# Attention into a mixture of experts: softmax exponentials head by head on ScalarE in the first ten chunks, with new opening plans

## The chip, the cores and the metric

One core of a Trainium2 chip runs the whole program. The metric is device time in microseconds (us) of one execution. Five engines work side by side, each through its own list of instructions: TensorE (PE), VectorE (DVE), ScalarE (ACT), GpSimd (POOL) and SyncE (SP), whose queue issues most DMA transfers.

## What is computed

For each of 8 batches, 8 heads of 576 queries attend to 72 keys and values, which are means over 8 neighbours:

```python
k_p = k.reshape(B, H, Sp, pool, D).mean(axis=3)
v_p = v.reshape(B, H, Sp, pool, D).mean(axis=3)
scores = scale * np.matmul(q, k_p.transpose(0, 1, 3, 2))
scores = scores - np.max(scores, axis=-1, keepdims=True)
attn = np.exp(scores)
attn = attn / (np.sum(attn, axis=-1, keepdims=True) + 1e-09)
return np.matmul(attn, v_p)
```

The 4608 rows of 512 numbers then go through a mixture of experts. A router picks one of 4 groups and one of 4 experts in it for each row, the row goes through that expert alone, `relu(x @ w1) @ w2` with 1024 hidden units, and the result is scaled by the two router weights.

## The kernel before

The work is cut into batches, and a batch's 576 rows into 5 chunks (four of 128 rows and one of 64). While the expert layer of batch b runs, the attention of batch b+1 is made ready, and the loads of batch b+2 start. Nearly all rows of a batch go to one expert, whose weights are loaded whole; the few other rows are done at the end in blocks of 32, one block straight in the last plan and the rest in a loop, which may run zero times.

The order of all work is written by hand in four strings of pieces: `START` and `FIRST` (batch 0 and the attention of batch 1), `STEADY` (used for batches 1 to 6) and `LAST`. A piece such as `a.ex:2` is a method call: `a` is the attention of the current batch, `n` of the next, `x` of the one after, `m` and `w` are the expert layers of the current and next batch, `t` is filler, `l` the leftover rows. Each engine runs its instructions in list order. The built order, taken per engine, can put a piece that is ready early ahead of a neighbour in the string.

The pieces of one attention chunk, with their lines:
- `sc` (L335): PE forms the scores of 8 heads, 72 columns each, in the PSUM tile `sc`, of which there is one buffer (two banks).
- `mx` (L341): DVE takes the maximum of every head. `sb` (L348 in batch 0, two instructions of L352 later): DVE subtracts it and writes `p` to SBUF, which sets `sc` free. `ex` (L357): ACT takes the exponential of all 576 columns at once. `su_` (L362 to L364): DVE sums each head, adds 1e-9 and inverts.
- `nm` (L372, L375): POOL multiplies by the inverse, first for `px` (16 keys of every second head), then for all of `p`.
- `px_`, `pm` (L380, L399): PE transposes; `pxa`, `pma` (L385, L387, L404): ACT copies them, rounded, to `pr` and `ph`; `pxd`, `pmd` (L392, L408): DVE forms the remainders.
- `av` (L417): PE multiplies with the values, for a half of the batch (chunks 0 and 1, or 2 to 4) at a time; `ava`, `avd` (L420, L424): ACT and DVE store result and remainder in `xt`.

The expert layer: `m.load` (L583) brings a tile of weights, `m.split` (L590, ACT) rounds it, `m.spd` (L595, POOL or DVE) takes the remainder; `m.up` (L608) is 12 matmuls, `ua` (L613, ACT) and `upd` (L618, DVE) empty its PSUM; `m.down` (L647) is 8 matmuls, `da` (L660) scales and stores. In the last batch `m.half` (L627) does one chunk in two halves; the first is emptied and stored by ACT, the second by DVE (L633) and SP's queue (L634).

`t.warm:z` (L920) is z matmuls whose result nobody reads, to keep PE busy while it would wait. `l.fetch_a`, `l.fetch_b` and `l.fetch_x` (L822, L827, L818) are SP's ten loads for the next block of leftover rows; they have a condition in a register and move nothing where no block follows. `l.slots` (L778 to L795) is DVE's preparation of that block, and `l.down` ends in an indirect store by POOL (L883).

Of the kernel before, what the change touches and what calls it, by code (L numbers as in the profile page):

```python
# [34 lines left out]
a.load_r:v a.load_k:1:w a.kr:1:v t.warm:1 a.load_k:0:w t.load_wr a.load_v:0 a.kr:0:p t.warm:7 a.load_r:k a.load_v:1 a.load_q:0 a.vr:0:v a.rr:v  # L35
t.warm:11 a.load_q:1 t.warm:20 n.load_r:v a.kb a.vr:1:v a.kt n.load_r:k a.kta a.guess_x a.load_q:2 a.qt:0 a.qta:0 a.vmain a.guess_e a.sc:0 a.rcopy
m.load:1:1 a.qt:1 t.warm:2 a.vrem a.qta:1 a.qt:2 a.sc:1 a.mx:0 a.sb:0 a.ex:0 a.su_:0 a.nm:0:p a.mx:1 t.warm:4 a.vm:0 a.vrx a.sb:1 a.load_q:3 a.px_:0
m.load:1:3 a.pxa:0 a.vm:1 a.pm:0 a.pma:0 t.warm:1 t.warm:5 a.pxd:0 a.ex:1 a.pmd:0 a.av:1:0:128 a.av:2:0:128 m.load:1:2 a.av:0:0:128 a.su_:1 a.qta:2
a.ava:1:0:128 a.ava:2:0:128 a.ava:0:0:128 a.avd:1:0:128 a.avd:0:0:128 a.av:3:0:128 n.load_k:0 m.load:1:0 n.load_k:1 a.nm:1:p n.load_v:0 a.ava:3:0:128
m.split:1:1 a.sc:2 t.warm:1 a.pm:1 a.avd:3:0:128 a.load_q:4 a.mx:2 n.load_qb:2 a.px_:1 n.load_qb:0 a.qt:3 a.pxa:1 t.warm:3 a.avd:2:0:128 a.pma:1  # L40
a.sb:2 a.ex:2 a.pxd:1 m.split:1:0 a.pmd:1 m.spd:1:0:p a.su_:2 a.av:2:128:128 a.qta:3 a.ava:2:128:128 a.av:0:128:128 a.sc:3 n.load_qb:3 a.ava:0:128:128
a.av:1:128:128 a.av:3:128:128 a.ava:1:128:128 a.ava:3:128:128 a.avd:2:128:128 a.avd:0:128:128 a.avd:3:128:128 a.avd:1:128:128 m.up:0:0 m.spd:1:1:v
# [3 lines left out]
a.mx:4 a.pma:2 a.sb:4 a.ex:4 a.pmd:2 m.up:2:0 m.split:1:3 t.warm:3 m.up:4:0 m.ua:2:0 a.nm:3:p m.load:2:1 a.pm:3 m.load:2:0 m.upd:1:0 a.px_:3 a.su_:4
a.nm:4:p m.ua:4:0 a.pxd:2 m.up:3:0 a.pxa:3 a.px_:4 a.pma:3 a.pxa:4 a.pxd:3 m.upd:2:0 a.pmd:3 a.pm:4 a.pxd:4 a.pma:4 m.split:2:1 a.pmd:4 a.av:3:256:320
a.av:2:256:320 m.upd:4:0 m.ua:3:0 a.ava:2:256:320 n.load_qb:1 x.load_k:0 a.ava:3:256:320 m.split:2:0 m.up:5:0 m.spd:1:3:v a.av:1:256:320 x.load_r:v
a.av:0:256:320 a.avd:2:256:320 a.ava:1:256:320 n.kr:0:r m.up:6:0 a.ava:0:256:320 a.avd:1:256:320 a.avd:3:256:320 m.ua:6:0 n.rr:p n.kr:1:p m.ua:5:0
m.spd:2:0:p m.load:2:2 a.avd:0:256:320 a.rt m.upd:3:0 m.upd:6:0 n.kt m.up:1:1 n.kta n.qb:0 m.upd:5:0 n.load_v:1 n.qb:1 n.sc:0 m.up:7:0 a.route  # L50
m.load:2:3 n.mx:0 n.rcopy n.sb:0 n.qb:2 m.ua:7:0 a.count n.ex:0 m.spd:2:1:p n.su_:0 m.ua:1:1 n.sc:1 n.nm:0:p m.up:0:1 n.mx:1 m.up:2:1 n.vrem m.ua:0:1
m.upd:7:0 a.gex n.sb:1 n.sc:2 m.upd:0:1 n.ex:1 m.upd:1:1 n.su_:1 n.px_:0 n.pm:0 n.mx:2 m.up:3:1 n.pxa:0 n.nm:1:p m.ua:2:1 m.up:4:1 x.load_k:1 m.ua:3:1
n.qb:3 n.px_:1 n.sb:2 x.load_qb:2 n.ex:2 n.pxd:0 x.load_r:k n.qb:4 m.split:2:2 m.upd:2:1 n.pxa:1 n.vrx a.gates n.pm:1 n.sc:3 n.vr:1:p n.mx:3 m.up:5:1
# [918 lines left out]
```

## Time and profile before

| | |
|---|---|
| median of 3 runs | 576.86 us (576.35 to 577.75) |
| the profiled execution's own time | 574.12 us |
| its span, first to last instruction | 572.4 us |
| mean granted TensorE clock | 0.990 of full speed |
| batches 1 to 6, each | 64.6 us |

The span is what the views below describe, from 0 to 572.4 us. The profiled execution took 1.7 us more than its span, and 2.7 us less than the median of the other runs. The opening (`START`) reaches to the first expert matmul at 35.4 us, `FIRST` to about 116 us; then the same 64.6 us come six times.

### The profile page before, as it was taken

What the parts mean: (1) busy time and instruction counts of PE and PEld (TensorE: products, weight loads), DVE (VectorE), ACT (ScalarE), POOL (GpSimd) and SP (SyncE); (2) the same over time, 40 slices, a digit from 0 to 9 for tenths busy, and PEclk for the clock granted to TensorE, in tenths of its full rate; (3) what the DMA queues carried; (4) which work ended last, traced back from release to release, by engine and by line L of the source; (5) the groups of instructions that cost most, each with busy time, mean ns of one, the idle gap of its engine ahead of it and who ended that gap; (6) DMA issues with size and microseconds to landing.
All of it is one profiled execution on the core that took longest, in us unless ns stands there. A gap on an engine that the chain in (4) does not pass through costs nothing. (4 is left out here: it accounts for less than half of the span.)

```text
span 572.4 us, 13094 instructions
## 1 busy us (share of the span) xinstructions
PE 558.0 (97%) x4896; PEld 497.4 (87%) x4896; DVE 397.5 (69%) x1075; ACT 273.9 (48%) x621; POOL 302.5 (53%) x301
## 2 busy tenths in 40 slices
...
GB/s 214 198 211 206 59 120 66 222 116 219 93 122 185 111 177 56 223 76 206 107 117 191 113 174 56 223 236 187 95 97 211 74 2 19 238 84 89 386 69 44
DMA packets 119362, 81.45 MB, mean 142 GB/s; under 512 B 76790, under 2 KB 95990, under 8 KB 118912
## 3 DMA queue, kind: packets, MB, share of 16 engines
...
q14 instruction: 26, 0.21, 0.1%
...
## 5 line engine op out<-in xcount | busy, mean ns | idle before, releaser
L608 PE MATMUL mm<-xt,w 128*128 128x320 f32 (+1 forms) x1536 | 221.1, 300 | 0.8 <-DVE ht L618 0.5
L608 PEld LDWEIGHTS mm<-xt,w 128*128 128x128 f32 x1536 | 208.2, 190 | 2.6 <-issue 0.7
L647 PE MATMUL mm<-w,ht 128*128 128x512 f32 x744 | 180.1, 395 | 0.0
L647 PEld LDWEIGHTS mm<-w,ht 128*128 128x128 f32 x744 | 136.9, 188 | 29.5 <-issue 1.8
L595 POOL TENSOR_TENSOR w<-sw,w 128x1024 fp32r<-128x1024 f32 x47 | 113.4, 2429 | 36.1 <-ACT w L590 36.1
L613 ACT ACTIVATE ht<-mm 128x320 fp32r<-128x320 f32 (+1 forms) x128 | 50.0, 410 | 61.9 <-PE mm L608 60.7
L618 DVE SCALAR_TENSOR_TENSOR ht<-mm,ht 128x256 fp32r<-128x256 f32 (+1 forms) x192 | 60.3, 348 | 24.7 <-ACT ht L613 23.8
L660 ACT ACTIVATE y<-mm,gm 128x512 f32<-128x512 f32 x31 | 21.2, 684 | 105.1 <-PE mm L647 105.1
L590 ACT CAST w<-sw 128x1024 fp32r<-128x1024 f32 x64 | 65.7, 1049 | 8.1 <-DMA sw<-in_moe_w_dram 8.1
L372 POOL TENSOR_TENSOR px<-p,su 128x128 f32<-128x128 f32 (+1 forms) x40 | 17.1, 427 | 67.7 <-DVE su L364 58.1
L272 POOL TENSOR_TENSOR rp<-rp,rh 32x128 f32<-32x128 f32 x8 | 3.6, 454 | 90.8 <-DMA rp<-rp 74.3
L431 POOL TENSOR_TENSOR sw<-xt 128x256 f32<-128x256 f32 (+1 forms) x56 | 43.7, 806 | 13.3 <-DVE xt L424 13.2
L375 POOL TENSOR_TENSOR p<-p,su 128x576 f32<-128x576 f32 (+1 forms) x40 | 46.0, 1151 | 3.1
L424 DVE TENSOR_TENSOR xt<-tp,xt 128x320 fp32r<-128x320 f32 (+2 forms) x68 | 28.1, 435 | 13.0 <-ACT xt L420 12.2
L420 ACT CAST xt<-tp 128x320 fp32r<-128x320 f32 (+2 forms) x68 | 25.4, 386 | 23.8 <-PE tp L417 22.5
L357 ACT ACTIVATE p<-p 128x576 f32<-128x576 f32 (+1 forms) x40 | 27.3, 682 | 16.9 <-DVE p L352 15.1
L362 DVE TENSOR_REDUCE su<-p 128x8 f32<-128x576 f32 (+1 forms) x40 | 29.9, 747 | 6.5 <-ACT p L357 5.4
L335 PEld LDWEIGHTS sc<-kT,qT 64*64 64x64 f32 x1264 | 24.0, 136 | 10.0 <-issue 4.8
L227 POOL TENSOR_TENSOR kv<-kv 128x512 f32<-128x512 f32 x20 | 32.5, 1624 | 0.2
L341 DVE TENSOR_REDUCE mx<-sc 128x8 f32<-128x576 f32 (+1 forms) x40 | 29.6, 740 | 3.0 <-PE sc L335 2.6
L335 PE MATMUL sc<-kT,qT 64*64 64x72 f32 x1264 | 30.0, 233 | 1.4 <-DVE p L352 1.0
L408 DVE TENSOR_TENSOR pl<-tp,ph 128x512 fp32r<-128x512 f32 (+1 forms) x40 | 25.2, 630 | 8.5 <-ACT ph L404 8.4
...
## 6 DMA issues: line engine op xcount, KB each, us to landing
...
```

The lines of the kernel that those rows point to most:

```text
L227: add(out=a[:, :, 0:256], in0=a[:, :, 0:256], in1=a[:, :, 256:512], op=ALU.add)
L335: nc.tensor.matmul(ps[t:t + 64, y, SP * g:SP * g + SP], lhsT=s.qT[c][r, g, t:t + 64], rhs=k, start=True, stop=True)
L341: red(out=mx[0:n], in_=scv, axis=AX.X, op=ALU.max)
L362: red(out=su[0:n], in_=s.p[c][0:n], axis=AX.X, op=ALU.add)
L375: eng.tensor_tensor(out=p[0:n], in0=p[0:n], in1=su[0:n].unsqueeze(3).broadcast_to([n, 2, 4, SP]), op=ALU.mult)
L431: nc.gpsimd.tensor_tensor(out=s.xw[g][:, sl], in0=s.xt[:, 0, g, sl].bitcast(F32), in1=s.xt[:, 1, g, sl].bitcast(F32), op=ALU.add)
L590: nc.scalar.copy(out=wh, in_=raw)
L595: (nc.vector if eng == "v" else nc.gpsimd).tensor_tensor(out=wl, in0=raw, in1=wh.bitcast(F32), op=ALU.subtract)
L608: nc.tensor.matmul(ps[:, 0:n], lhsT=l[:, kc, fs], rhs=xt[:, r, kc, sl], start=(kc == 0 and i == 0), stop=(kc == 3 and i == 2))
L613: nc.scalar.activation(out=s.ht[f][:, o:o + n], in_=s.pu[f, hf][:, 0:n], func=AF.Relu)
L618: stt(out=ht[:, at:at + hi - lo], in0=ps[:, lo - o:hi - o], scalar=0.0, in1=ht[:, lo:hi].bitcast(F32), op0=ALU.max, op1=ALU.subtract)
L647: nc.tensor.matmul(ps, lhsT=s.ht[f][:, 640 * l + o:640 * l + o + 128], rhs=s.w[2, f // 2][r][:, f % 2, :], start=(i == 0), stop=(i == 23))
```

## The change

Three things change.

1. `mx`, `ex` and `su_` get a second form, `h`. `mx` in this form writes the negative maximum. `ex` makes no use of `sb`: it reads the scores from PSUM, and takes eight ACT instructions of 72 columns, one for each head, with the negative maximum as bias and with `accum_out`, which leaves the head's sum in `su`. `su_` then has only the addition and the inversion left. The form `h` is used for chunks 2, 3 and 4 of batch 0 and chunks 1 to 4 of batch 1, seven of the first ten chunks.
2. `START` and `FIRST` are new tables with the same pieces, but without the seven `sb`, with 49 filler matmuls for 58 (34, 8, 4 and 3), and with some pieces on another engine: `spd:1:1` of batch 0 and of batch 1 go from DVE to POOL, `spd:1:2` from POOL to DVE, `n.vr:0` from POOL to DVE as one reduction, `x.kr:0` and `x.vr:0` from DVE reductions to POOL additions, `x.rr` from a DVE reduction to DVE additions; `a.kr:0` goes to DVE, `a.vr:0` to POOL. The loads at the start stand in a new order.
3. In `LAST`, `l.fetch_x`, `l.slots` and `l.fetch_b` now come ahead of the second half of the last chunk.

```diff
-m.down:8 m.da:4 l.up m.da:2 m.half:3:0 l.hback l.fetch_a l.down m.half:3:1 l.slots l.fetch_b l.fetch_x
+m.down:8 m.da:4 l.up m.da:2 m.half:3:0 l.hback l.fetch_a l.fetch_x l.down l.slots l.fetch_b m.half:3:1
...
-        def mx(s, c):
+        def mx(s, c, how="v"):
...
-            red(out=mx[0:n], in_=scv, axis=AX.X, op=ALU.max)
+            red(out=mx[0:n], in_=scv, axis=AX.X, op=ALU.max, negate=how == "h")
...
-        def ex(s, c):
-            n, p = s.span(c)[1], s.p[c]
-            nc.scalar.activation(out=p[0:n], in_=p[0:n], func=AF.Exp)
-
-        def su_(s, c):
+        def ex(s, c, how="v"):
             n = s.span(c)[1]
+            if how == "v":
+                nc.scalar.activation(out=s.p[c][0:n], in_=s.p[c][0:n], func=AF.Exp)
+                return
+            p = s.p[c] = sm.tile([128, 2, 4, SP], F32, name="p")
             su = s.su[c] = sm.tile([128, 2, 4], F32, name="su")
-            red(out=su[0:n], in_=s.p[c][0:n], axis=AX.X, op=ALU.add)
+            for i in range(4):
+                for y in range(2):
+                    z, k = (i // 2, 2 * y + i % 2) if s.b else (i // 2, 2 * (i % 2) + y)
+                    nc.scalar.activation(out=p[0:n, z, k], in_=s.ss[c][0:n, y, SP * i:SP * i + SP], func=AF.Exp,
+                                         bias=s.m[c][0:n, y, i:i + 1], accum_out=su[0:n, z, k:k + 1])
+
+        def su_(s, c, how="v"):
+            n = s.span(c)[1]
+            if how == "v":
+                s.su[c] = sm.tile([128, 2, 4], F32, name="su")
+                red(out=s.su[c][0:n], in_=s.p[c][0:n], axis=AX.X, op=ALU.add)
+            su = s.su[c]
             ts(out=su[0:n], in0=su[0:n], scalar1=1e-9, scalar2=None, op0=ALU.add)
             nc.vector.reciprocal(out=su[0:n], in_=su[0:n])
```

How the instructions move is seen at three places. In the changed kernel every line behind `ex` has a number 11 higher (L601 for L590, L415 for L404 and so on).

ACT in `START`, between the second chunk's copies (`pr`, `ph`) and the last stores to `xt` ahead of the first expert matmul, before:

```order
L385 CAST pr<-tp 96x128
L387 CAST pr<-tp 32x128 x2
L404 CAST ph<-tp 128x4x128
L357 ACTIVATE p<-p 128x576
L590 CAST w<-sw 128x1024
L320 COPY qT<-tp 128x512
L420 CAST xt<-tp 128x128 x4
L590 CAST w<-sw 128x1024
```

and now:

```order
L601 CAST w<-sw 128x1024
L415 CAST ph<-tp 128x4x128
L396 CAST pr<-tp 96x128
L398 CAST pr<-tp 32x128 x2
L365 ACTIVATE p,su<-sc,mx 128x72 x8
L601 CAST w<-sw 128x1024
L320 COPY qT<-tp 128x512
L431 CAST xt<-tp 128x128 x2
L601 CAST w<-sw 128x1024
L431 CAST xt<-tp 128x128 x2
```

The one exponential of chunk 2 (L357) has become eight (L365), which stand ahead of the rounding of the weight tile (L590, now L601) that the first expert matmul needs; one more weight tile stands between the stores to `xt`.

POOL at the same place, before:

```order
L372 TENSOR_TENSOR px<-p,su 128x128
L375 TENSOR_TENSOR p<-p,su 128x576
L595 TENSOR_TENSOR w<-sw,w 128x1024
L372 TENSOR_TENSOR px<-p,su 128x128
L375 TENSOR_TENSOR p<-p,su 128x576
L227 TENSOR_TENSOR kv<-kv 128x2x256
```

and now:

```order
L383 TENSOR_TENSOR px<-p,su 128x128
L386 TENSOR_TENSOR p<-p,su 128x576
L383 TENSOR_TENSOR px<-p,su 128x128
L386 TENSOR_TENSOR p<-p,su 128x576
L606 TENSOR_TENSOR w<-sw,w 128x1024 x2
L383 TENSOR_TENSOR px<-p,su 128x128
```

The two products of chunk 2 (`px` and `p`, now L383 and L386) have moved ahead of the remainder of the first weight tile (L595, now L606), and the remainder of a second weight tile stands right behind it.

SP at the end of `LAST`, where L634 (now L645) is the last store of the output, before:

```order
L822 DMA sw<-in_moe_w_dram 128x4x256
L634 DMA out_dram<-y 128x256
L827 ISA
L827 DMA kv<-in_moe_w_dram 128x2x512
L827 ISA
L827 DMA kv<-in_moe_w_dram 128x2x512
L827 ISA
L827 DMA kv<-in_moe_w_dram 128x2x512
L827 ISA
L827 DMA rem<-in_moe_w_dram 128x2x512
L818 ISA
L818 DMA ph<-xscr 128x2304
```

and now:

```order
L829 DMA ph<-xscr 128x2304
L829 ISA
L829 DMA pl<-xscr 128x2304
L838 ISA
L838 DMA kv<-in_moe_w_dram 128x2x512
L838 ISA
L838 DMA kv<-in_moe_w_dram 128x2x512
L838 ISA
L838 DMA kv<-in_moe_w_dram 128x2x512
L838 ISA
L838 DMA rem<-in_moe_w_dram 128x2x512
L645 DMA out_dram<-y 128x256
```

The store stood ahead of six conditional loads and is now behind all of them.

## Rows read from the trace of the kernel before

**Rows 1.** Page, part 1: engine busy us (share of the span) xinstructions.
```profile
PE 558.0 (97%) x4896; PEld 497.4 (87%) x4896; DVE 397.5 (69%) x1075; ACT 273.9 (48%) x621; POOL 302.5 (53%) x301
```

**Rows 2.** Busy time by stage: stretch, its us, engines (xinstructions), TensorE clock, DMA share, GB/s.
```profile
15.10:21.90 6.80, 6.80 (x76) 6.05 (x78) 3.35 (x10) 3.78 (x9) 1.17 (x2) 0.50 0.31 78
35.40:48.40 13.00, 12.06 (x103) 10.58 (x102) 11.24 (x22) 8.82 (x24) 12.03 (x13) 1.00 0.75 157
48.40:62.40 14.00, 12.84 (x197) 11.94 (x197) 13.19 (x34) 5.33 (x13) 9.14 (x7) 1.00 0.77 218
62.40:90.80 28.40, 27.25 (x277) 23.90 (x278) 26.24 (x78) 18.83 (x49) 17.64 (x20) 1.00 0.34 66
116.40:181.00 64.60, 64.60 (x559) 57.73 (x558) 46.48 (x118) 33.80 (x78) 37.63 (x36) 1.00 0.52 150
```

**Rows 3.** Groups of ACT to 117 us: count, busy us, mean ns, idle.
```profile
L357 ACT ACTIVATE p<-p 128x576 f32<-128x576 f32 x10 | 6.8, 682 | 2.0 <-DVE p L352 1.9
L387 ACT CAST pr<-tp 32x128 fp32r<-32x128 f32 x16 | 4.1, 257 | 0.2
L277 ACT ACTIVATE vx<-rp,sel 96x128 fp32r<-96x128 f32 x6 | 2.1, 391 | 0.0
L420 ACT CAST xt<-tp 128x128 fp32r<-128x128 f32 x8 | 2.0, 269 | 2.1 <-PE tp L417 2.1
```

**Rows 4.** The same of DVE.
```profile
L362 DVE TENSOR_REDUCE su<-p 128x8 f32<-128x576 f32 x10 | 7.4, 742 | 1.4 <-ACT p L357 1.2
L352 DVE TENSOR_TENSOR p<-sc,mx 128x288 f32<-128x288 f32 x12 | 4.9, 447 | 0.3
L348 DVE TENSOR_TENSOR p<-sc,mx 128x576 f32<-128x576 f32 x4 | 3.0, 755 | 0.2
```

**Rows 5.** Timeline of ACT: start us, us, instruction [idle before].
```profile
10.69 1.28 ACT L250 ACT_TABLE_LOAD   x1 [10.69 <-DMA wr<-in_moe_w_expert_dram]
12.38 0.40 ACT L250 COPY rp<-rp 32x256 f32<-32x256 f32 x1 [0.40 <-DVE rp L232]
21.82 0.68 ACT L277 ACTIVATE vx<-rp,sel 96x128 fp32r<-96x128 f32 x2
24.39 0.91 ACT L266 ACTIVATE vml<-vp,sel 128x256 fp32r<-128x256 f32 x2
25.32 0.58 ACT L404 CAST ph<-tp 128x512 fp32r<-128x512 f32 x1
32.26 1.03 ACT L590 CAST w<-sw 128x1024 fp32r<-128x1024 f32 x1
47.98 0.37 ACT L404 CAST ph<-tp 128x256 fp32r<-128x256 f32 x1
```

**Rows 6.** Timeline of POOL around the first weight tile.
```profile
33.37 2.37 POOL L595 TENSOR_TENSOR w<-sw,w 128x1024 fp32r<-128x1024 f32 x1 [3.86 <-ACT w L590]
35.70 0.40 POOL L372 TENSOR_TENSOR px<-p,su 128x128 f32<-128x128 f32 x1
36.18 1.15 POOL L375 TENSOR_TENSOR p<-p,su 128x576 f32<-128x576 f32 x1
```

**Rows 7.** Timeline of PE: filler matmuls, and a stalled score group.
```profile
41.89 0.83 PE L920 MATMUL mm<-ones 128*128 128x128 f32 x6
62.43 0.73 PE L335 MATMUL sc<-kT,qT 64*64 64x72 f32 x32 [1.02 <-DVE p L352]
```

**Rows 8.** Timeline of SP's DMA issues at the end.
```profile
566.58 0.37 SPq L634 DMA_DIRECT2D out_dram<-y  x1
567.29 0.91 SPq L827 DMA_DIRECT2D kv<-in_moe_w_dram  x3
569.34 0.07 SPq L818 DMA_DIRECT2D pl<-xscr  x1
```

**Rows 9.** SP's waits at the end: total us, times, longest.
```profile
SPq L634 <- DMA out_dram<-q,idx: 8.4, 1, 8.4
```

**Rows 10.** Line 634, the half stores: issue to landing.
```profile
DMA to landing us min/median/max: 1.7/1.7/1.7
```

More of the change, by code (lines that the diff above doesn't have):

```diff
@@ L34 @@
 START = """
[L35 to L42, printed above, removed]
+t.warm:12 a.load_k:0:w a.load_r:v a.load_k:1:w a.load_v:0 a.kr:0:v a.load_r:k a.kr:1:v t.warm:9 a.vr:0:p a.load_v:1 a.rr:v a.load_q:0 t.load_wr
@@ new lines @@
+a.load_q:1 a.load_q:2 a.kb t.warm:13 a.vr:1:v a.kt n.load_r:k a.kta a.guess_x a.vmain a.qt:0 a.qta:0 a.guess_e a.rcopy a.sc:0 a.qt:1 n.load_r:v a.mx:0
+a.sb:0 m.load:1:1 a.qta:1 m.load:1:2 a.qt:2 a.sc:1 t.warm:8 a.ex:0 a.su_:0 a.mx:1 m.load:1:3 a.vrem a.nm:0:p a.qta:2 n.load_k:0 a.sb:1 a.vm:1 a.vrx
+a.load_q:3 a.px_:0 a.pm:0 a.vm:0 a.pxa:0 a.pma:0 a.pxd:0 a.pmd:0 m.load:1:0 a.sc:2 t.warm:4 a.av:1:0:128 n.load_k:1 a.ex:1 a.av:3:0:128 a.av:2:0:128
+a.ava:1:0:128 a.ava:2:0:128 a.su_:1 n.load_v:0 a.av:0:0:128 a.nm:1:p a.avd:1:0:128 a.ava:3:0:128 a.load_q:4 a.pm:1 n.load_qb:2 a.px_:1 a.ava:0:0:128
@@ L46 @@
[L46 to L53, printed above, removed]
@@ L62 @@
[L62 to L63 removed]
+m.ua:0:0 m.up:1:0 a.mx:3:h a.nm:2:p a.ex:3:h a.qt:4 n.vr:0:r m.spd:1:1:p a.px_:2 m.upd:0:0 m.spd:1:2:v a.su_:3:h a.nm:3:p a.qta:4 a.pm:2 a.pxa:2
+a.sc:4 a.mx:4:h a.pma:2 m.split:1:3 m.ua:1:0 m.up:2:0 m.up:4:0 m.load:2:1 a.ex:4:h m.ua:2:0 m.upd:1:0 a.pmd:2 a.px_:3 a.pm:3 a.su_:4:h a.pxa:3 a.pxd:2
@@ new lines @@
+a.pma:3 m.up:3:0 m.ua:4:0 a.nm:4:p a.px_:4 a.pmd:3 a.pxa:4 a.pm:4 a.pxd:3 m.load:2:0 a.pxd:4 a.pma:4 a.pmd:4 a.av:2:256:320 m.split:2:1 m.upd:4:0
+a.av:3:256:320 n.kr:1:p m.split:2:0 m.up:5:0 a.ava:3:256:320 a.av:0:256:320 a.av:1:256:320 a.ava:2:256:320 n.load_qb:1 m.upd:2:0 n.rr:p m.ua:5:0
+m.spd:1:3:v a.ava:0:256:320 m.up:6:0 a.avd:2:256:320 a.ava:1:256:320 n.kr:0:r m.ua:3:0 a.avd:1:256:320 a.avd:0:256:320 m.ua:6:0 a.avd:3:256:320
+m.load:2:2 n.kt a.rt n.load_v:1 m.upd:3:0 x.load_k:1 x.load_r:k m.upd:5:0 m.upd:6:0 n.kta m.up:1:1 m.load:2:3 n.qb:1 n.qb:0 n.rcopy x.load_k:0 n.sc:0
@@ new lines @@
+n.ava:0:256:320 n.av:1:256:320 n.av:3:256:320 n.avd:0:256:320 n.ava:1:256:320 n.av:2:256:320 x.kr:0:p n.ava:3:256:320 n.xr:2:0:256 n.xr:0:0:256
+n.avd:1:256:320 n.xr:3:0:256 n.xr:1:0:256 m.down:3 n.avd:3:256:320 n.xr:1:256:320 n.ava:2:256:320 n.xr:3:256:320 n.avd:2:256:320 m.da:0 n.xr:0:256:320
+m.down:4 x.rr:v n.xr:2:256:320 n.rt m.down:5 n.route x.kr:1:p m.da:1 x.kt m.down:6 n.gex n.main_expert x.kta m.down:7 x.sc:0 n.gates w.load:1:0
+x.rcopy w.load:1:2 x.vrem x.mx:0 x.vr:0:p x.sb:0 m.down:8 x.qb:1 x.ex:0 m.da:2 x.su_:0 m.down:13 m.da:4 m.down:9 x.nm:0:p w.load:1:3 w.split:1:0
```

23 lines of the change are left out of this document (12 added, 11 removed).

## The prediction

> **What bounds the kernel now.** I read the page's busy shares first, then a table of busy time by stage, then the timelines where PE has idle time, and last SP's queue at the end. PE is busy for 97% of the span, DVE for 69%, ACT for 48% [rows 1]. PE's list has a fixed order and nearly fixed work, so time can be won only where PE idles, or before its first and behind its last real matmul. The stage table tells where that is: 64.60 of 64.6 us busy in a steady batch, which the change doesn't touch, but idle times of 0.94 us at 35.4 to 48.4, 1.16 at 48.4 to 62.4 and 1.15 at 62.4 to 90.8 [rows 2]. The reader is to see which engine is full there: DVE with 13.19 of 14.0 us and then 26.24 of 28.4, while ACT has 5.33 and 18.83. The group of scores at 62.43 waits 1.02 us for DVE's subtraction, since `sc` has one buffer [rows 7]. So DVE paces the opening, and ACT has room. At the end PE has stopped and SP alone goes on [rows 8].
>
> **The price of one chunk in the new form.** DVE loses its sum, 0.74 us, and its subtraction, 0.76 in batch 0 and at most 2 x 0.45 in batch 1 [rows 4]: 1.5 us a chunk, 10.5 in all. ACT loses one exponential of 0.68 and gains eight of 72 columns [rows 3]. The nearest row is the masked copy of L277, also with an operand for each partition: 0.39 us alone, two in 0.68, so start to start 0.29 for 128 columns [rows 3, 5]. A column costs about (682 - 269) / (576 - 128) = 0.92 ns [rows 3], so 72 columns take 0.24 start to start and 0.34 alone: 7 x 0.24 + 0.34 = 2.0 us, 1.3 more than now, 9.1 in all. No row shows an accumulated sum. It can't cost less than nothing, as the eight do all that the row does; above, it could be a further short ACT instruction behind each, 0.26 each as the 32x128 copies [rows 3], 2.1 a chunk and 4.1 us together. I take the lower end, since L277 differs by the sum alone and the copies are whole instructions, and keep 4.1 for the range.
>
> From scores to inverted sum the chain of a chunk loses 0.76 + 0.68 + 0.74 = 2.18 us and gets 2.0: 0.2 shorter, if ACT is free when the maximum is there.
>
> **START.** The loads come in another order, keys first. DVE then reaches the sum that ACT's copy at 12.38 waits for (0.40 idle, released by DVE) sooner, and the copy goes behind the table load, which ends at 10.69 + 1.28 = 11.97: 0.4 us won [rows 5]. Two masked copies (24.39, 0.91 us) no longer stand straight ahead of the first `ph` at 25.32 [rows 5]; that can give up to 0.9, and I take 0.35, as the POOL product before it moves only with the 0.4. Against this stand the eight exponentials of chunk 2, ahead of the rounding of the first weight tile: it ended at 32.26 + 1.03 = 33.29 and now ends at 33.29 - 0.75 + 1.3 = 33.85. Next is POOL's list: the remainder of that tile ran from 33.37 to 35.74, and PE's second expert matmul needs it; now the two products of chunk 2, 0.40 + 1.15 us, go first [rows 6]. Their sums are inverted at about 33.3, so they end near 34.9 and the remainder at 34.9 + 2.37 = 37.3. **START is 1.5 us slower.** What was hidden under the same wait (two stores to `xt` behind a further rounding on ACT) stays hidden: without that cover it would add about one rounding, 1.0 us [rows 5]. The filler matmuls removed from START cost nothing either way, since PE waits there for others.
>
> **FIRST up to 48.4 us.** The six records of filler at 41.89 go: 0.83 us of PE [rows 7]. Chunks 3 and 4 are on the chain to the `ph` that ended at 47.98 + 0.37 = 48.35 [rows 5], each 0.2 shorter. ACT takes 2 x 1.3 = 2.6 us more into its 13.00 - 8.82 = 4.2 us of room [rows 2]. 1.5 - 0.8 - 0.4 leaves **0.3 late**. The weight remainders that change place (one DVE to POOL, one POOL to DVE) and the moved pooling sums pass under expert matmuls whose tiles are not yet due.
>
> **48.4 to 90.8 us.** To the scores at 62.43 nothing is changed in kind: the first chunk of batch 1 keeps the old form. Behind them four chunks are 0.2 shorter each, 0.8, and PE's idle time to be won is 1.15 [rows 2]; I take **0.6 won**. The cover is ACT's room: 18.83 + 4 x 1.3 = 24.0 of 28.4 us, 85%, less than DVE's 92% now. After 90.8 and in the steady batches PE idles nowhere [rows 2], so the sums that change engine there are free; if a later stage lost that cover, the nearest price is one POOL remainder, 2.4 us [rows 6].
>
> **The end.** SP issues the last store at 566.58, then six conditional loads, the last at 569.34 + 0.07 = 569.41, and the program ends 3.0 us later at 572.4 [rows 8]. The store is held 8.4 us on SP by the landing of POOL's indirect store [rows 9], not by DVE, so it can't come earlier; what is queued behind it on SP, and then all engines at the loop's exit, wait for it. The six loads now fit into those 8.4 us. SP is then done at 566.95, 2.46 us earlier. But the exit must see the store land, 1.7 us after issue [rows 10], at 568.3: if that was the first thing asked, 568.3 + 3.0 = 571.3 and 1.1 are won; if the last, all 2.46. I take the middle, **1.8 won**. DVE's preparation of the next block moves under PE's last matmuls.
>
> **Sum.** 1.5 - 0.8 - 0.4 - 0.6 - 1.8 = -2.1 us: the profiled execution (574.12, span 572.4) would become 572.0, its span 570.3. That execution lies 2.7 below the median; set against the median, 576.86 - 2.1 = **574.8 us**. A measurement of this kernel tells about 0.3%, 1.7 us, from no change.
>
> The Trainium skill, "ScalarE: Activation LUTs", Rules for kernel authors, budgets about 0.3 us and 0.83 ns an element for each ACTIVATE with a pointer bias. By that a chunk would cost 8 x 0.36 = 2.9 us and the sum come out near 579; no row here has the instruction, and L277's pairs, at 0.29 for 128 columns, speak against it.
>
> **Rivals.**
> - *ScalarE becomes the bound (slower).* The place is 62.4 to 90.8, and chunks 2 to 4 before it. With the middle of my bounds, 3.0 us a chunk, ACT has 18.83 + 4 x 2.3 = 28.1 of 28.4 us [rows 2], and each chunk holds the only `sc` buffer until its eighth exponential. Each further us a chunk costs 1 in START, 2 on chunks 3 and 4, and about half of 4 behind: 5 us. At 3.0: 574.8 + 5 = 579.8. It decides from 2.0 + 2.1 / 5 = 2.4 us a chunk (no gain), and from 2.8 the kernel is slower by over 0.3%. For it: no row prices the sum. Against: L277.
> - *The upper bound holds.* At 4.1 us, 18.83 + 4 x 3.4 = 32.5 us of ACT don't fit into 28.4: 2.1 x 3 + 4.1 = 10.4 more, 585.2.
> - *DVE's release is worth more.* If DVE paced all three stretches, their idle time of 3.25 us goes in place of the 1.0 of shorter chains: 1.5 - 0.8 - 3.25 - 1.8 = -4.35, 572.5. For it: DVE's 94% and 92%; against: waits for POOL and ACT stand among them.
> - *The clock.* PE ran at half its clock, 1.2 GHz, from 15.1 to 21.9 [rows 2], behind filler and very small matmuls. The new plan has less filler there. If that lasts as long again, half of 6.8 us of matmuls at worst, 3.4, and with PE waiting in part about 2: 576.8, no change.
>
> **How the numbers follow.** Forecast 0.37 (its own range 573.0 to 576.5), ScalarE bound 0.27, upper bound 0.10, more from DVE 0.19, clock 0.07. Faster by over 0.3% (below 575.1): two thirds of the forecast, 0.24, and DVE's 0.19: 0.43. Within: 0.13 of the forecast, 0.06 of ScalarE's lower part, 0.06 of the clock: 0.25. Slower: 0.21, 0.10 and 0.01: 0.32. The range reaches from below DVE's case, 571.0, to 582.5, above the middle price; it leaves out the upper bound and some of the lowest.
>
> **What would show it.** Eight exponentials from first start to last end: 2.0 us, or 3 and more. The first weight remainder on POOL ends near 37.3. The scores that stood at 62.43 come 0.3 later, and wait for ACT in place of DVE. ACT is about 85% busy from there to the end of batch 1's chunks. SP's last issue is the store, and the span ends about 4 us behind it. The prediction is wrong if a chunk's eight take over 2.4 us, if PE's idle time up to 90 us grows, or if a steady batch is no longer 64.6 us.

## The result, and the profile after

| | before | after |
|---|---|---|
| median of 5 runs each, side by side | 576.68 us (575.62 to 577.75) | 584.49 us (583.14 to 584.65) |
| ratio | | 1.0142, 95% interval 1.0122 to 1.0162 |
| the profiled execution | 574.12, span 572.4 | 584.65, span 583.0 |
| mean granted TensorE clock | 0.990 | 0.976 |

The changed kernel is **slower by 1.4%**. The forecast, 574.8 us, had the wrong sign, and its range (571.0 to 582.5) doesn't hold the result. The loss arises ahead of the first steady batch, which begins 11.8 us late and is then as long as before. The busy shares of the page and the table by stage answer to [rows 1, 2], over the same times of the span:

```profile
PE 562.3 (96%) x4878; PEld 502.4 (86%) x4878; DVE 385.9 (66%) x1057; ACT 285.4 (49%) x726; POOL 307.4 (53%) x305
```

```profile
15.10:21.90 6.80, 6.57 (x71) 6.07 (x72) 2.25 (x10) 2.62 (x7) 0.73 (x1) 0.58 0.38 74
21.90:35.40 13.50, 11.45 (x124) 10.04 (x124) 8.78 (x21) 10.06 (x27) 3.57 (x5) 0.75 0.85 273
35.40:48.40 13.00, 12.23 (x108) 11.31 (x107) 6.47 (x15) 9.10 (x43) 6.63 (x5) 0.69 0.45 131
48.40:62.40 14.00, 12.26 (x82) 11.58 (x83) 9.23 (x19) 10.90 (x37) 9.88 (x10) 0.88 0.83 195
62.40:90.80 28.40, 24.30 (x350) 22.05 (x349) 22.25 (x72) 18.39 (x79) 14.13 (x14) 1.00 0.36 81
128.20:192.80 64.60, 64.60 (x559) 57.73 (x559) 46.37 (x117) 35.13 (x81) 40.07 (x38) 1.00 0.54 150
```

A steady batch is 64.60 us as before. The rows up to 90.8 can't be compared one by one with those of before, since the work stands later in them. The stretch of before from 62.40 opens with the second score group of batch 1 (62.43 [rows 7]); after, that group comes at 71.77. The first of the two rows below goes from there to 10.77 us behind the scores of chunk 4, as that stretch of before did, and has the same work on PE (27.25 us before). The second goes from the scores of chunk 2 to those of chunk 4:

```profile
71.77:102.71 30.94, 27.37 (x278) 23.98 (x279) 21.64 (x67) 25.38 (x109) 18.61 (x21) 1.00 0.30 57
76.93:91.94 15.01, 12.48 (x139) 11.41 (x139) 11.62 (x38) 14.03 (x58) 9.79 (x12) 1.00 0.46 75
```

So DVE did get its room (21.64 us for 26.24), and ACT took its place: 25.38 of 30.94 us, 82%, where 24.0 of 28.4 were forecast, and 14.03 of 15.01, 93%, between those two score groups. The same work takes 2.5 us more. PE's clock is at its lower level, 1.2 GHz, in three stretches of the opening; two of them in rows of the same view:

```profile
16.20:26.40 10.20, 10.20 (x109) 9.39 (x110) 4.84 (x15) 5.00 (x11) 1.95 (x4) 0.50 0.30 80
33.20:43.40 10.20, 9.12 (x68) 8.25 (x67) 4.41 (x13) 6.99 (x27) 5.21 (x4) 0.50 0.45 139
```

The third is short, 57.1 to 60.5. Before there was one, 15.1 to 21.9 [rows 2].

The lateness is best followed on PE's timeline. The table gives the start of score groups and of the first expert matmul in the profiled executions (us; "first up" is that matmul, m.up:0:0, and x.sc:1 opens the first steady plan):

| kernel | a.sc:0 | a.sc:2 | a.sc:3 | first up | a.sc:4 | n.sc:0 | n.sc:4 | x.sc:1 |
|---|---|---|---|---|---|---|---|---|
| before | 17.4 | 28.5 | 33.8 | 35.4 | 39.7 | 58.9 | 80.0 | 116.4 |
| after | 20.5 | 28.1 | 40.8 | 42.0 | 47.6 | 67.6 | 91.9 | 128.2 |
| lateness | +3.1 | -0.5 | +7.0 | +6.5 | +7.9 | +8.8 | +11.9 | +11.8 |

(The lateness is taken from the times before rounding.) Such a table holds chance too. In e10_nofill, whose lists are those of before but for six filler matmuls and whose time is the same, the first expert matmul comes at 35.4, n.sc:0 at 61.6 and x.sc:1 at 119.5. So the columns up to the first expert matmul hold, and from n.sc:0 on some 3 us can be chance.

Three places of it. First the start: the sum of the remainder rows on DVE, the copy of it on ACT, and PE's transposes behind it (timelines of the three engines; before, the copy began at 12.38 [rows 5]):

```profile
12.26 1.25 DVE L227 TENSOR_TENSOR rem<-rem 64x512 f32<-64x512 f32 x1 [1.73 <-DMA wr<-in_moe_w_expert_dram]
13.55 0.83 DVE L228 TENSOR_TENSOR rem<-rem 64x256 f32<-64x256 f32 x1
14.88 0.40 ACT L250 COPY rp<-rp 32x256 f32<-32x256 f32 x1 [1.10 <-DVE rp L232]
15.33 0.44 PE L293 MATMUL tp<-ident,rp 128*128 128x128 f32 x2 [3.62 <-ACT rp L250]
```

In the new order DVE sums both key tiles first and then waits 1.73 us. The profile puts this down to the load that it saw land last, `wr`; in e16_opening, which has the same START, the same wait, 1.76 us, is put down to the rows themselves. Its two additions then take 1.25 and 0.83 us in place of 0.69 and 0.42, while POOL's sum of the values, moved there by the change, runs beside them. PE stands for 3.62 us.

Second, ACT and POOL around chunk 2, which answer to [rows 5, 6]:

```profile
28.56 0.59 ACT L415 CAST ph<-tp 128x512 fp32r<-128x512 f32 x1
...
34.90 0.32 ACT L365 ACTIVATE p<-sc,mx 128x72 f32<-128x72 f32 x1
35.11 0.19 ACT L365 ACTIVATION_READ_ACCUMULATOR p<-sc,mx 128x1 f32 x1
35.21 0.31 ACT L365 ACTIVATE p<-sc,mx 128x72 f32<-128x72 f32 x1
...
37.19 0.24 ACT L365 ACTIVATION_READ_ACCUMULATOR p<-sc,mx 128x1 f32 x1
37.28 1.08 ACT L601 CAST w<-sw 128x1024 fp32r<-128x1024 f32 x1
38.22 0.64 ACT L320 COPY qT<-tp 128x512 f32<-128x512 f32 x1
```

```profile
38.60 1.15 POOL L386 TENSOR_TENSOR p<-p,su 128x576 f32<-128x576 f32 x1
39.71 4.71 POOL L606 TENSOR_TENSOR w<-sw,w 128x1024 fp32r<-128x1024 f32 x2
```

The eight exponentials run from 34.90 to 37.43, 2.53 us. Behind them stand the rounding of the first weight tile and the copy of chunk 3's queries; and the tile's remainder on POOL, from 33.37 before, starts at 39.71. Most of that was late already: the first `ph` begins at 28.56 (25.32 before [rows 5]), 3.2 us late, and so do the exponentials.

Third, batch 1. From its first scores to those of its chunk 4 the changed kernel takes 24.3 us, the kernel before 21.1 and e10_nofill 21.4: 3 us are lost here, most of it where ACT is 93% full. PE waits 0.27 and 0.67 us for ACT's `p` ahead of the scores of chunks 2 and 3, and 1.39 and 0.47 us for expert matmuls to be emptied, the first of them on ACT at 85.82, late in its list:

```profile
87.01 1.99 PE L619 MATMUL mm<-xt,w 128*128 128x320 f32 x12 [1.39 <-DVE ht L629]
```

### The profile page after: what moved, and what is told of

Read it like the earlier page. It is cut to its first block, busy times and chain, and to the rows that moved or that the text cites. A ratio compares the mean times of both kernels' runs of the same rounds, so it can differ in the third digit from the quotient of the medians.

```text
span 583.0 us, 13160 instructions
## 1 busy us (share of the span) xinstructions
PE 562.3 (96%) x4878; PEld 502.4 (86%) x4878; DVE 385.9 (66%) x1057; ACT 285.4 (49%) x726; POOL 307.4 (53%) x305
## 5 line engine op out<-in xcount | busy, mean ns | idle before, releaser
L658 PE MATMUL mm<-w,ht 128*128 128x512 f32 x744 | 180.1, 395 | 0.0
L606 POOL TENSOR_TENSOR w<-sw,w 128x1024 fp32r<-128x1024 f32 x48 | 116.4, 2442 | 31.7 <-ACT w L601 31.6
L624 ACT ACTIVATE ht<-mm 128x320 fp32r<-128x320 f32 (+1 forms) x128 | 50.0, 411 | 58.4 <-PE mm L619 57.3
L601 ACT CAST w<-sw 128x1024 fp32r<-128x1024 f32 x64 | 65.5, 1048 | 1.6 <-DMA sw<-in_moe_w_dram 0.9
L383 POOL TENSOR_TENSOR px<-p,su 128x128 f32<-128x128 f32 (+1 forms) x40 | 16.3, 408 | 67.8 <-DVE su L375 58.4
L386 POOL TENSOR_TENSOR p<-p,su 128x576 f32<-128x576 f32 (+1 forms) x40 | 46.1, 1152 | 3.1
L435 DVE TENSOR_TENSOR xt<-tp,xt 128x320 fp32r<-128x320 f32 (+2 forms) x68 | 28.4, 436 | 20.1 <-ACT xt L431 19.3
L431 ACT CAST xt<-tp 128x320 fp32r<-128x320 f32 (+2 forms) x68 | 25.4, 388 | 22.7 <-PE tp L428 21.1
L358 ACT ACTIVATE p<-p 128x576 f32<-128x576 f32 x33 | 22.5, 682 | 24.0 <-DVE p L352 23.8
L663 PE MATMUL mm<-w,ht 128*128 128x512 f32 x128 | 30.9, 391 | 0.0
```

The source lines that it names most:

```text
L386: eng.tensor_tensor(out=p[0:n], in0=p[0:n], in1=su[0:n].unsqueeze(3).broadcast_to([n, 2, 4, SP]), op=ALU.mult)
L601: nc.scalar.copy(out=wh, in_=raw)
L606: (nc.vector if eng == "v" else nc.gpsimd).tensor_tensor(out=wl, in0=raw, in1=wh.bitcast(F32), op=ALU.subtract)
L624: nc.scalar.activation(out=s.ht[f][:, o:o + n], in_=s.pu[f, hf][:, 0:n], func=AF.Relu)
L658: nc.tensor.matmul(ps, lhsT=s.ht[f][:, 640 * l + o:640 * l + o + 128], rhs=s.w[2, f // 2][r][:, f % 2, :], start=(i == 0), stop=(i == 23))
L663: nc.tensor.matmul(ps, lhsT=s.ht[f][:, 512:640], rhs=s.w[2, f // 2][r][:, f % 2, :], start=(i == 0), stop=(i == 15))
```

## Experiments

Each is compared with runs of the kernel before on the same chip, and the ratio is to those. Single runs of the kernel before spread from 572.8 to 578.7 us over all sets, and its profiled execution, 574.12, is one of the shorter; so the ratios decide, and the profiles tell where.

### The parts of the change alone

**e1_end**: part 3 alone.

```diff
-m.down:8 m.da:4 l.up m.da:2 m.half:3:0 l.hback l.fetch_a l.down m.half:3:1 l.slots l.fetch_b l.fetch_x
+m.down:8 m.da:4 l.up m.da:2 m.half:3:0 l.hback l.fetch_a l.fetch_x l.down l.slots l.fetch_b m.half:3:1
```

> The kernel before with part 3 of the change alone (the new order at the end of LAST). All theories: everything up to the last plan as before, the first scores of the steady plan at 116.4 us, SP's last issue the store. The prediction's term for the end, -1.8, gives about 574.9 us against 576.7 before; what the two profiles leave over (+11.8 us at the start of STEADY, +10.6 at the end of the span) says -1.2, 575.5. If the six late loads had been hidden: 576.7.

Measured: 1.0005 (0.9982 to 1.0027), no difference; the 1.8 us of the forecast (0.9969) lie outside this interval. The loads did move: SP's last one is at 562.66, and the store, still held, is last.

```profile
562.66 0.07 SPq L827 DMA_DIRECT2D rem<-in_moe_w_dram  x1
566.65 0.37 SPq L634 DMA_DIRECT2D out_dram<-y  x1
```

The span ends 4.9 us behind the store's end (571.9 - 567.02), for 5.45 before (572.4 - 566.95 [rows 8]): 0.6 won in these two executions, of the 1.8 that I took.

**e2_form**: the new form alone, in the plans of before.

```diff
-... a.mx:2 ... a.sb:2 a.ex:2 ... a.su_:2
+... a.mx:2:h ... a.ex:2:h ... a.su_:2:h
```

(the same for the other six chunks.)

> The plans of before, with the form h put in for the seven chunks and their sb left out; nothing else of the change. Theory FORM (the eight exponentials of 2.5 us hold sc and ScalarE, and that is the loss): start of STEADY 124 to 129 us, time 583 to 588. Theory PLANS (the new opening tables are the loss: late sums of the keys, gaps on TensorE, and the lower clock behind them; the form by itself is about even): start of STEADY 114 to 119, time 575 to 579, first scores at 17.4 as before.

**e3_plans**: the new plans, with all chunks in the old form.

```diff
-... a.mx:2:h a.pxa:1 a.ex:2:h ... a.su_:2:h
+... a.mx:2 a.sb:2 a.pxa:1 a.ex:2 ... a.su_:2
```

> The changed kernel's plans, but every chunk in the old form (subtraction and sum on VectorE, one exponential). Theory FORM: most of the 11.8 us goes, start of STEADY 116 to 120, time 575 to 579. Theory PLANS: the first scores stay at 20.5 us, TensorE's granted clock is again at half from 16 to 26 us and later, start of STEADY 124 to 129, time 582 to 587.

**e4_start**: the change with the START of before, in the form h.

```diff
-START = """ t.warm:12 a.load_k:0:w a.load_r:v a.load_k:1:w a.load_v:0 a.kr:0:v
+START = """ a.load_r:v a.load_k:1:w a.kr:1:v t.warm:1 a.load_k:0:w t.load_wr
...
```

> The changed kernel with the START table of before (chunk 2 in the form h there too), and FIRST and LAST of the change; the two weight tiles that change tables go along. Theory PLANS, with the loss in START: first scores at 17.4, half clock only 15 to 22 us, start of STEADY 115 to 120, time 574 to 578. Theory FORM: chunk 2's exponentials still hold the weight tile and FIRST still loses, start of STEADY 122 to 127, time 580 to 585.

Measured: e2_form **1.0214** (1.0179 to 1.0250), e3_plans **1.0173** (1.0135 to 1.0210), e4_start 1.0157 (1.0122 to 1.0191). Both theories were too simple: each half loses by itself at least as much as the whole does (1.0142), and in the whole the two losses don't add up. But neither is a half as the change has it: e2_form puts the new form into plans laid for the old one, e3_plans the old form into plans laid for the new one. In e4_start the first expert matmul is 2.2 us late, and 5.7 more are lost from there to x.sc:1, in the new FIRST with the form h.

| kernel | a.sc:0 | a.sc:3 | first up | a.sc:4 | n.sc:0 | n.sc:4 | x.sc:1 |
|---|---|---|---|---|---|---|---|
| before | 17.4 | 33.8 | 35.4 | 39.7 | 58.9 | 80.0 | 116.4 |
| e2_form | 17.2 | 35.9 | 38.4 | 46.4 | 65.1 | 87.7 | 126.9 |
| e3_plans | 19.9 | 40.5 | 41.7 | 47.7 | 65.3 | 92.0 | 127.9 |
| e4_start | 16.5 | 34.7 | 37.6 | 44.3 | 64.3 | 88.0 | 124.3 |

### Why the form loses in the plans of before

**e5_b0** and **e6_b1**: the form on batch 0's three chunks alone, and on batch 1's four alone (same edits as e2_form, on those chunks).

> Plans of before, the form h on chunks 2 to 4 of batch 0 alone. Theory QUEUE (in the form h it is ScalarE's list that lets the sc buffer go, and the exponentials of chunk 3 stand there behind the emptying of the first expert matmul, which itself waits for the first weight tile's remainder): nearly the whole loss of the form alone is here, scores of chunk 4 at 46 us for 39.7, start of STEADY 122 to 125, time 581 to 584 at a level of before of 574.4 to 576.7. Theory PRICE (each chunk loses about the same, 10.5 / 7 = 1.5 us): start of STEADY 121, time 579.

> Plans of before, the form h on chunks 1 to 4 of batch 1 alone. Theory QUEUE: up to 62 us as before; then 0 to 4 us lost, start of STEADY 116 to 120, time 575 to 579. Theory PRICE: 4 x 1.5 = 6 us lost, start of STEADY 122, time 581. My prediction's term for these chunks was 0.6 us won.

Measured: e5_b0 1.0107 (1.0078 to 1.0137), e6_b1 1.0081 (1.0054 to 1.0109). The two intervals overlap, and PRICE's loss by the number of chunks, 4.5 and 6 us (1.0078 and 1.0104), lies in or at the edge of both; so these two runs don't part the theories, and e9_queue and e12_again below have to. Together the two lose 1.88%, within the interval of e2_form. ACT in e5_b0, and PE:

```profile
33.92 1.09 ACT L601 CAST w<-sw 128x1024 fp32r<-128x1024 f32 x1
...
42.75 0.38 ACT L624 ACTIVATE ht<-mm 128x256 fp32r<-128x256 f32 x1 [2.82 <-PE mm L619]
43.03 0.32 ACT L365 ACTIVATE p<-sc,mx 128x72 f32<-128x72 f32 x1
```

```profile
35.55 1.24 PE L335 MATMUL sc<-kT,qT 64*64 64x72 f32 x32 [2.25 <-ACT qT L320]
...
38.49 0.73 PE L619 MATMUL mm<-xt,w 128*128 128x256 f32 x2
40.00 5.07 PE L619 MATMUL mm<-xt,w 128*128 128x256 f32 x22 [0.78 <-POOL w L606]
```

Chunk 2's exponentials hold up the weight tile's rounding (32.26 before [rows 5]) and, behind it, the copy of chunk 3's queries, for which PE waits 2.25 us (0.39 before). The expert matmuls start 3.1 us late, the third of them waits 0.78 us more for the remainder on POOL, and at 1.2 GHz the other 22 take 5.07 us, where 24 took 3.25 before. The emptying of their PSUM tile (L624) stands on ACT **ahead** of chunk 3's exponentials, though their maximum is there since 37.6 us (DVE). So they start 5.4 us behind it, and POOL's product of them comes at 46.25 for 43.19. Before, `sb` on DVE set the one `sc` tile free whatever ACT waited for; here `sc` is held until 45.5. But chunk 4's scores (46.3 for 39.7) didn't wait for that: PE is in the expert matmuls until 45.1 and then in transposes, without a wait.

**e9_queue**, and **e12_again**, the same kernel once more: e5_b0 with ACT's list mended.

```diff
-... a.ex:2:h a.pxd:1 m.split:1:0 ... a.qta:3
+... a.qta:3 m.split:1:0 a.ex:2:h a.pxd:1
...
-m.split:1:2 a.nm:2:p m.up:1:0 a.mx:3:h m.ua:0:0 n.vr:0 a.qt:4 a.px_:2 a.ex:3:h
+a.mx:3:h a.ex:3:h m.split:1:2 a.nm:2:p m.up:1:0 m.ua:0:0 n.vr:0 a.qt:4 a.px_:2
```

> The form h on chunks 2 to 4 of batch 0 in the plans of before (as e5_b0), with ScalarE's list mended: the copy of chunk 3's queries and the rounding of the first weight tile ahead of chunk 2's exponentials, and chunk 3's exponentials ahead of the emptying of the first expert matmul. Theory QUEUE (the exponentials are dear by what they stand behind and ahead of on ScalarE): first expert matmul 36 to 37.5 us for 38.5, chunk 4's scores at 41 to 43 for 46.3, start of STEADY 118 to 121 for 124.0, time within 3 us of before. Theory PRICE (2.5 us of exponentials for 0.7 are dear wherever they stand): start of STEADY 122 to 125, time 4 to 8 us above before.

> The kernel of e9 once more, since its profiled execution (584.33 us) lay 6.6 above the median of its eleven and can't show where the others spent their time. Theory QUEUE: a profile near 577.7, first expert matmul at 36 to 38, start of STEADY 117 to 120. Theory PRICE: the mended list gives nothing that lasts, start of STEADY 122 or later again.

Measured: 1.0037 (1.0016 to 1.0058) and 1.0042 (1.0019 to 1.0065), where e5_b0 had 1.0107. The same exponentials at the same price, and six tenths of their loss is gone with the order of a few entries (with it POOL does the remainder ahead of chunk 2's products again, as before, where e5_b0 had it behind them). ACT in e12_again, and PE:

```profile
32.17 1.06 ACT L601 CAST w<-sw 128x1024 fp32r<-128x1024 f32 x1
33.11 0.34 ACT L365 ACTIVATE p<-sc,mx 128x72 f32<-128x72 f32 x1
...
40.84 0.36 ACT L365 ACTIVATE p<-sc,mx 128x72 f32<-128x72 f32 x1
...
42.27 0.38 ACT L624 ACTIVATE ht<-mm 128x256 fp32r<-128x256 f32 x1
```

```profile
35.71 1.24 PE L335 MATMUL sc<-kT,qT 64*64 64x72 f32 x32 [2.26 <-ACT p L365]
```

Chunk 3's last exponential (40.84) is now ahead of the emptying. What is left: chunk 3's scores wait 2.26 us for ACT's `p`, which holds `sc` here, and start at 35.7 for 33.8, and the first expert matmul comes at 38.65, later than I expected, since PE takes those scores first. Whether the whole remaining 0.4% is the price of the exponentials no run takes apart.

Batch 1's loss, in e6_b1, shows in PE's waits. It stands 0.98 and 0.64 us for ACT's `p` ahead of the scores of chunks 2 and 3, and then the eight exponentials of chunk 4 (88.67 to 91.1) stand on ACT ahead of chunk 3's copies:

```profile
93.26 0.39 PE L429 MATMUL tp<-ph,vmh 128*128 128x256 f32 x1 [1.40 <-DVE pl L420]
```

### Why the plans lose

**e15_first** and **e16_opening**: the new FIRST alone, and the new START alone, all chunks in the old form.

> Every chunk in the old form; the START of before, the FIRST and the LAST of the change (two weight tiles go along with their tables). If the new FIRST by itself carries a loss: first expert matmul at 35.4 as before, then 3 to 6 us lost up to STEADY, time 579 to 582. If the losses seen behind 42 us were only the late opening carried on: time 575 to 577.

> Every chunk in the old form; the START of the change, the FIRST and LAST of before. If the new START carries about half of the plans' loss: first expert matmul at 41 to 42, no more lost behind it, time 580 to 583. If its lateness is taken up behind it: 576 to 579.

**e17_loads**: e16_opening with the loads and key sums of before. **e18_scores**: e17_loads, and chunk 3's scores where before has them.

```diff
-t.warm:12 a.load_k:0:w a.load_r:v a.load_k:1:w a.load_v:0 a.kr:0:v a.load_r:k a.kr:1:v
+a.load_r:v a.load_k:1:w a.kr:1:v t.warm:1 a.load_k:0:w t.load_wr a.load_v:0 a.kr:0:p
...
-t.warm:3 a.av:0:128:128 a.av:1:128:128 ... a.av:3:128:128 a.sc:3
+t.warm:3 a.sc:3 a.av:0:128:128 a.av:1:128:128 ... a.av:3:128:128
```

(The first pair is e17_loads; e18_scores has both.)

> e16 with the first part of START as before, up to the keys' copies, and chunk 2's query load right behind the guess. Theory LOADS: first scores at 17.4, first expert matmul 2.5 to 3.5 us sooner than in e16, time 2 to 4 below e16. If what waits behind is as late anyway: first expert matmul within 1 us of e16.

> e17 with chunk 3's scores ahead of three of the four products of the second half, as before has them. If the place of those scores on TensorE was the rest of START's loss: first expert matmul at 35.5 to 36.5, time within 1.5 us of before. If other work of START holds it: first expert matmul above 37.

| kernel | ratio | a.sc:0 | a.sc:3 | first up | n.sc:0 | x.sc:1 |
|---|---|---|---|---|---|---|
| e15_first | 1.0057 (1.0030 to 1.0084) | 16.9 | 33.5 | 35.8 | 60.0 | 122.3 |
| e16_opening | 1.0111 (1.0072 to 1.0150) | 20.3 | 41.6 | 42.8 | 67.7 | 126.1 |
| e17_loads | 1.0058 (1.0036 to 1.0079) | 17.0 | 39.3 | 40.5 | 65.8 | 123.1 |
| e18_scores | 1.0033 (1.0014 to 1.0052) | 16.7 | 34.3 | 38.3 | 62.4 | 119.9 |

Here the parts add up within their intervals: 0.57% of FIRST and 1.11% of START make 1.68%, and both together had 1.73% (e3_plans). Of START's 1.11%, the loads are about half, 0.53% (no run of e16_opening is as short as the longest of e17_loads, on the same chip); e17_loads puts filler and chunk 2's query load back as well. The place of chunk 3's scores, behind all products of the second half, is another 0.25%, 2.0 us between the medians on that chip. What holds the last 0.33% was not taken apart. In e18_scores the first expert matmul is 2.8 us late, and PE works from 31.9 to 38.3 us without a wait, at 1.2 GHz, with six filler matmuls (1.5 us) among its work; before, the same products took until 35.4. So there the clock and the filler stay open as the cause. In FIRST the loss shows in PE's waits from 35.4 us on (waits of e15_first; total, times, longest):

```profile
PE mm L620 <- DVE ht L630: 3.4, 2, 2.5
```

Before, that wait was 0.5 us in all. The longest, 2.5 us, is for an emptying on DVE at 80.02, which stands behind the maximum, both subtractions and the sum of chunk 3 (77.30 to 80.10). Subtractions and sum aren't in the change's own form, where the same kind of wait is 1.39 and 0.47 us, behind ACT. So e15_first doesn't show what FIRST costs in the change itself.

### The clock

**e7_fill**, **e13_clock**: more filler in the changed START, in e13_clock (whose diff this is) only into PE's waits.

```diff
-... a.kb t.warm:13 ... a.pm:1 ... a.qt:3 ... t.warm:3 a.av:0:128:128
+... a.kb t.warm:37 ... t.warm:3 a.pm:1 ... t.warm:3 a.qt:3 ... a.av:0:128:128
```

> The changed kernel with 51 more filler matmuls in START, all where its TensorE waited: 25 behind the 34 of the opening, 26 around the first products with the values and ahead of the scores of chunk 3. Theory CLOCK (the lost half of TensorE's clock at 16 to 26 and 33 to 43 us carries most of the lateness of the opening): half clock under 10 us in all up to 62 us in place of 23.9, the first expert matmul 3 to 6 us sooner than 41.97, time 578 to 581. Theory CHAIN (the lateness is the chain of sums, exponentials and weight remainders on the other engines; TensorE waits for them whatever its clock): first expert matmul at 40 to 43, start of STEADY 126 to 130, time 583 to 587.

> The changed kernel with filler only where TensorE stood still: 24 matmuls more ahead of the first copies of the keys (the 3.6 us wait), 3 more ahead of chunk 1's transposes (a wait of 0.96), and the 3 that stood between the second half's products moved to the wait of 1.08 ahead of chunk 3's queries. Theory CLOCK: the stretch from 33 to 43 us keeps the full clock, the first expert matmul comes at 38 to 39.5 for 42.0, start of STEADY 122 to 125, time 578 to 581. Theory CHAIN: the clock is back, but TensorE waits for ScalarE's exponentials and copy instead; first expert matmul 40.5 to 42.5, time 582 to 585.

Measured: e7_fill 1.0196 (1.0162 to 1.0230), e13_clock 1.0195 (1.0156 to 1.0233). No gain; whether it is a loss can't be told, since the intervals touch that of the change. In e7_fill some filler stood in the way (chunk 1's transposes at 34.92 for 32.80), so e13_clock is the test. Its clock (table by stretch):

```profile
15.10:21.90 6.80, 6.45 (x90) 5.58 (x88) 2.42 (x11) 2.93 (x7) 0.73 (x1) 1.00 0.28 65
21.90:38.40 16.50, 11.65 (x142) 10.13 (x142) 9.24 (x25) 13.47 (x44) 4.89 (x7) 1.00 0.81 256
38.60:45.30 6.70, 6.70 (x58) 6.44 (x59) 4.33 (x6) 2.36 (x13) 4.69 (x3) 0.50 0.35 100
```

Full clock up to 38.4 us, and the scores of chunk 2 at 27.2 for 28.1, the first expert matmul at 40.62 for 41.97: 1.4 of the 6.5 us, and 0.6 of it was there at the first scores. PE idles for 4.9 of the 16.5 us in place of being slow: it waits 1.37 us for DVE, 0.82 for POOL, 0.47 for DVE and 2.17 for ACT's copy of chunk 3's queries. So from 16 to 38 us the lower clock explains at most those 1.4 us. It then comes later, where PE doesn't wait: the 24 expert matmuls take 5.21 us for 3.79 in the change. At x.sc:1 e13_clock is still 1.3 us ahead of the change (126.9 for 128.2), and one batch later no more (193.1 for 192.8); so x.sc:1 alone doesn't tell the time of these kernels.

### Mended versions of the whole

**e8_loads** (the change with the loads and key sums of before), **e11_fix** (that, ACT's list mended as in e9_queue, and chunk 3's scores earlier), **e14_both** (e11_fix with filler at its waits).

> The changed kernel with the first part of START as before, up to the copies of the keys (order of loads and filler, the sums of keys and values on the engines of before); all behind it as in the change. Theory LOADS (the remainder rows' sum comes 2.5 us late by the new order, and that carries through): first scores at 17 to 17.5 for 20.5, start of STEADY 124 to 126, time 580 to 582. Theory CHAIN: first scores as early, but the first expert matmul is still 4 us or more behind that of before, at 39.5 to 42, and the time 582 to 585.

> The changed kernel mended at three places: the opening of START up to the keys' copies as before, chunk 2's query load right behind the guess as before; the copy of chunk 3's queries and the rounding of the first weight tile ahead of chunk 2's exponentials; the scores of chunk 3 ahead of the second half of the products with the values, and its exponentials ahead of the emptying of the first expert matmul. Theory QUEUE: first expert matmul at 37 to 39 us for 42.0, chunk 4's scores at 42 to 44 for 47.6, start of STEADY 120 to 123, time 577 to 580. Theory CLOCK: the granted clock decides still; with the same products in a new order the half-clock stretches stay at 24 us and the time at 582 or more.

> The mended changed kernel of e11 with filler at its three waits as well (5 ahead of chunk 1's transposes, 5 ahead of chunk 3's queries in place of the 3 behind, 10 ahead of chunk 3's scores). If list order and clock are both needed: first expert matmul 37 to 39 for 41.2 in e11, start of STEADY 118 to 122, time 576 to 579. If the clock is no cause of its own: as e11, 583 to 585.

Measured: 1.0174 (1.0140 to 1.0207), 1.0148 (1.0115 to 1.0180), 1.0171 (1.0131 to 1.0211); all misses. In e8_loads I had put chunk 2's query load too late, and PE waited 3.52 us for it at 22.39: it tells nothing on the loads (e17_loads does). In e14_both the scores of chunk 2 come at 24.9, 3.6 us ahead of before, and the first expert matmul still at 40.9. PE and DVE there:

```profile
39.97 0.47 PE L428 MATMUL tp<-ph,vmh 128*128 128x128 f32 x1 [1.89 <-DVE xt L435]
```

```profile
37.78 1.93 DVE L224 TENSOR_REDUCE vp<-kv 128x128 f32<-128x1024 f32 x1
```

The sum of the next batch's values, which the change gave to DVE, runs ahead of the store to `xt` that PE's product waits for. Three mends at places where the trace showed waits were not enough. e14_both, with filler in those waits, is no faster than e11_fix.

**e10_nofill**: the kernel before without the filler at 41.89 us.

```diff
-... m.split:1:3 t.warm:3 m.up:4:0
+... m.split:1:3 m.up:4:0
```

> The kernel before without one piece of filler, the six records at 41.89 us. The prediction's term: 0.83 us won. If TensorE waits there anyway: nothing. If the filler held TensorE's clock: half clock somewhere between 35 and 62 us, and 1 to 3 us lost.

Measured: 0.9994 (0.9970 to 1.0017): no difference. The 0.83 us of the forecast are 0.14% and would lie within this interval, so the time can't decide. In the trace PE waits where the filler was, and the next matmuls come 2.14 us after the last ones for 2.43, 0.3 us won:

```profile
43.37 1.70 PE L608 MATMUL mm<-xt,w 128*128 128x256 f32 x12 [0.44 <-DVE ht L618]
```

No kernel of these runs is measurably faster than before.

## Why the prediction was wrong, step by step

- **What bounds the kernel** was right where it was read: steady batches are untouched at 64.60 us, and all happens before x.sc:1. ACT's load was forecast well too: for the work of 62.4 to 90.8 ACT is busy for 25.38 us where I forecast 24.0, 82% where I forecast 85%. But a busy share doesn't say whether a wait is covered. At 82% in the mean ACT is 93% full for 15 us, and PE waits for it there.
- **The price of a chunk**, 2.0 us, was 2.53, inside the bounds. My slope of 5 us for each further us would have made 2.6 us of that, 577.4 us: a mis-sized term, and too small for the result.
- **START, +1.5 us: this step failed.** The first expert matmul came 6.5 us late (41.97 for 35.44 [rows 2]). The first `ph` was to come at 25.32 - 0.75 = 24.57 and came at 28.56, 3.2 us later than before. "0.4 us won" by the new loads was 2.5 us lost (the copy at 14.88 for 12.38; e17_loads against e16_opening: 0.53%). All that I had costed moved with it: the rounding of the weight tile ended at 38.36 for a forecast 33.85, and the remainder, which was to end at 37.3, began at 39.71. The first expert matmul came straight behind chunk 3's scores, at 40.80 for 33.83. The eight exponentials ahead of the weight tile I did see, but not that the copy of chunk 3's queries stands behind them too; in e5_b0 alone that made PE wait 2.25 us. And I costed nothing for chunk 3's scores having moved behind the products (0.25%, e18_scores against e17_loads). I read the order of POOL and ACT at one place, and not that of PE and SP.
- **Chunks 3 and 4, -0.4, and batch 1, -0.6**: the chain from scores to inverted sum was counted as a chain of durations. What counted was what stands behind the exponentials on ACT, and that they hold `sc` meanwhile (PE's waits: 2.25 us for a copy in e5_b0; 2.26 in e12_again, 0.98 and 0.64 in e6_b1 for `sc`). With the lists mended the loss of batch 0's chunks went from 1.07% to 0.4% (e5_b0, e12_again). This is the step behind the form's loss in the plans of before; in the change batch 1 lost 3 us in place of winning 0.6.
- **The filler, -0.8**: 0.3 us in the trace, and nothing that the time could show (e10_nofill).
- **The end, -1.8**: the loads moved as said, 0.6 us were won in the profiles, and no difference could be measured (e1_end).
- **The new plans as plans** had no term of their own beyond these, and lose 1.73% even with every chunk in the old form.
- **Rivals.** *ScalarE the bound* had the right sign and much of the mechanism: PE waits for `sc` until the eighth exponential (e12_again, e6_b1), and ACT is 93% full for 15 us of batch 1. But at the 2.53 us measured its own sum gives 577.4, and most of the lateness is there before batch 1, in START. *The clock* had chance 0.07: the stretches at 1.2 GHz did grow to 24 us in all, but a full clock up to 38 us won 1.4 of 6.5 us and no time (e13_clock). From the expert matmuls on no run tests it. *DVE's release* fell: DVE was released, 21.64 us for 26.24, and the time didn't gain by it.
- **What would show it**: a chunk over 2.4 us, and more idle time of PE up to 90 us. Two of the three signs of being wrong came. Of the others, ACT at about 85% (82), the store as SP's last issue with the end 4.7 us behind it (577.95, 583.0) and the steady 64.60 us came too. The remainder's end did not, and the scores of 62.43 came at 71.77, without a wait; it is chunks 2 and 3 that wait for ACT.

Open: the last third of START's loss, the details of FIRST's, and why form and plans don't add up. Between after (1.0142) and e3_plans (1.0173), whose intervals overlap, the form costs nothing that can be measured. In their two profiles the first expert matmul comes at 42.0 and 41.7; with the form n.sc:0 comes 2.3 us later (67.6 for 65.3), and n.sc:4 does not (91.9 for 92.0). No run shows why.
